# One fused attention and mixer kernel: the first K load ahead of the first Q load, and a new order of work with other engines for some small copies

## The chip, the cores and the metric

The kernel runs on one core of a Trainium2 chip. A core has five engines, each with its own instruction stream, and they meet only through semaphores. PE (TensorE) multiplies, DVE (VectorE), ACT (ScalarE) and POOL (GpSimd) do elementwise work, and SP (SyncE) here only issues transfers (DMAs). POOL also issues transfers. The metric is the device time of one execution in microseconds (us). The times shown are of three runs, and the profile is of one more execution.

## What is computed

Four batches of eight-head attention over 768 tokens with head size 64 are followed by a mixer. Cut to what matters, the reference is:

```python
scores = q @ k.T / 8 - slope[h] * dist          # per batch and head
keep   = (key < 8) | (0 <= query - key < 96)    # 8 global keys, 96 local ones
a      = softmax(where(keep, scores, -1e9))
x      = (a @ v), heads side by side            # 4 x 768 x 512
h      = x.T @ U @ V                            # over tokens, rank 32
u      = x + h.T
out    = u + relu(u @ w_ch1) @ w_ch2            # 512 -> 2048 -> 512
```

All inputs and the output are float32. The kernel computes in float16 with float32 sums.

## The kernel before, in words

**The units of work.** Heads are taken two at a time, so there are 16 pairs, pair p = 4 x batch + head pair. A query block of 128 tokens meets two key blocks: its own, and the one before it with its first 32 keys replaced by the global ones. This second form of K is kept in kO and that of V in vo. A task's name is a short code with the pair's number behind it, and a part behind a dot:

- lk, lq, lv: the loads of K, Q and V (function add_load, L389 to L444). Pair 0's K and Q are loaded as float32 by SP (L416) into stg32, which borrows the memory of the tile sA, and are cast to float16 by Ck0.0, Ck0.1, Cq0.0 and Cq0.1 (L421 to L433). All other loads are issued by POOL and cast on the way (L400, L404, L408).
- TK, TQ: transposes on PE (L518 to L560). EK, EQ: their results copied from PSUM to kT and qT by DVE or ACT. KO: the two copies that make kO (L583 to L609). VC and VG: the two copies that make vo, all keys and then the global ones (L614 to L626).
- SB: the position bias as a matmul, for the first batch alone (L640 to L651). S: the scores. EX: the exponential on ACT (L728). MK: the mask on DVE, for pairs 4 and up. PV: weights times values (L795, L796). RC and NM: the reciprocal and the normalising multiplication on DVE. XC: the cast of x to float16 (L858). UP: transposes and the first step of the mixer (L769 to L779). XE, XU, TE: the middle steps. HM: the last step of the mixer (L890), in a full-array or a half-array form. E0 and E1: the result copied to uT.
- M1a to M1d and RL: the first MLP product and its relu. ZP, ZU, ZW, ZX, ZA, ZB, ZD, ZQ, ZR, ZV, with ZT and ZS: a part of the first MLP in batches 1 to 3 done with seven products for eight. PA and PB: sums on DVE that let the second MLP be done the same way. RS, P1 to P7 and DA to DH: the second MLP and its additions into x_sb. O: the stores by SP.
- w1_0 to w1_3 and w2_0 to w2_3: the weights' loads, 512 KB each, by POOL. mixl: the loads of U and V of the mixer by SP. u16 and vs: copies of these.

**What sets the order.** The list ORDER names every task once, across all engines. A planner (class Planner, method run, L146 to L216) walks the list, gives each task a start time from costs written into the program, and picks the buffer that it uses: three for K and for Q, four for V, eight PSUM banks. The tasks are then emitted by start time. On any one engine this is the order of the list, so what decides on the chip is the list and the buffers; the planner's own times are not run. A task's engine comes from a letter in CFG (A for ACT, D for DVE, P for POOL, S for a transfer by SP): KO, VO (for VC and VG), EK, EQ, XC, TE, XE, E and so on, one letter for each pair.

**What follows for each queue.** An engine takes its tasks strictly in turn. POOL's stream holds the loads and its copies mixed, so a load can't be issued while POOL waits to begin a copy. LANES = 8 (L107) lets at most eight POOL transfers be in flight. V's four buffers are given by PV of an earlier pair, K's and Q's three by TK and TQ.

**Counting.** Each task has a fixed number of instructions on its engine (PV 22, UP 12, a P product 8, KO 2, VC 1). Counting them along the list gives every row of the trace its task.

**Idle matmuls.** Until the first M1a0.0, gaps on PE that the planner foresees are filled with matmuls on zeros (L1201).

Of the kernel before, what the change touches and what calls it, by code (L numbers as in the profile page):

```python
# [10 lines left out]
FP32 = mybir.dt.float32  # L11
# [10 lines left out]
ones2 ones0 wz lq0 iota lk1 ones3 lk0 vz relf rel3 bias1 bias0 bias2 lq1 Ck0.0 Ck0.1 Cq0.0 Cq0.1 SB0.1 lk2 lv0 lq2  # L22
TK0 EK0.1 EK0.0 KO0.0 TQ0 EQ0.0 EQ0.1 SB0.2 lk3 KO0.1 lq3 SB0.0 ones1 S0.0 TK1 EK1 back lv1 S0.2 S0.1 EX0.0 TQ1 EQ1
KO1 lk4 SB1.2 VC0 VG0 lv2 lv3 bias4 EX0.2 EX0.1 lq4 TK2 EK2 KO2 SB1.1 S1.1 EX1.1 S1.2 EX1.2 SB1.0 PV0 RC0 NM0 TQ2
EQ2 TK3 EK3 KO3 S1.0 SB2.1 VC1 VG1 lk5 SB2.2 S2.2 lq5 w1_0 mixl u16 EX1.0 TQ3 EQ3 XC0 EX2.2 SB2.0 S2.0 EX2.0 S2.1
EX2.1 PV1 RC1 VC2 VG2 NM1 VC3 VG3 vs1 vs0 XC1 SB3.1 S3.1 SB3.0 SB3.2 EX3.1 S3.0 S3.2 EX3.0 EX3.2 PV2 RC2 NM2 TK4 EK4
UP0 TQ4 w1_3 KO4 TE0 PV3.0 PV3.1 EQ4 HM0 E00 PV3.2 RC3.0 UP1 NH3.0 TE1 TK5 XC2 TQ5 EK5 KO5 w1_2 HM1 RC3.1 E01 RC3.2
NH3.2 UP3.0 NH3.1 UP3.1 UP3.2 EQ5 lk7 NM3 lv4 TE3 S4.2 UP2 TE2 HM3 E03 M1a0.3 EX4.2 S4.0 HM2 E02 E13 M1c0.3 M1a0.2
M1c0.2 lq6 EX4.0 S5.1 mask1 EX5.1 S4.1 EX4.1 M1d0.3 M1b0.3 RL0.3 lk6 M1d0.2 M1b0.2 RL0.2 w1_1 M1a0.14 VC4 M1a0.0
M1c0.0 M1d0.0 ZS6 mask0 MK4.0 M1b0.14 RL0.14 mask2 M1b0.0 M1a0.15 M1b0.15 TK7 M1a0.9 M1b0.9 EK7 KO7 lq7 M1a0.10  # L30
RL0.15 RL0.0 mask3 RL0.9 MK4.1 TD0 S5.0 EX5.0 w2_2 S5.2 VG4 EX5.2 M1b0.10 MK5.0 lv5 M1a0.11 MK5.1 M1a0.13 M1b0.11
TQ6 RL0.10 MK4.2 EQ6 TK6 RL0.11 M1b0.13 M1a0.7 M1b0.7 RL0.13 EK6 MK5.2 PA0.3 PV4 w2_0 RC4 TQ7 M1a0.6 M1b0.6 RL0.7
EQ7 M1a0.5 w2_1 PB0.3 M1a0.8 vs2 NM4 XC4 UP4 RL0.6 KO6 w2_3 XE4 M1b0.5 RL0.5 M1b0.8 RL0.8 PA0.1 M1a0.1 VC5 PB0.1 VG5
M1c0.1 M1d0.1 XU4 M1a0.4 TE4 HM4 TWa0 TWb0 E04 M1b0.4 RL0.4 M1b0.1 RL0.1 PV5 M1a0.12 M1b0.12 RL0.12 S6.2 RC5 NM5 lk8
RS0.0 S6.1 EX6.1 lq8 PA0.0 P10.0 PB0.0 lq9 PA0.2 mask4 PB0.2 P20.0 S7.0 mask7 TWa1 RS0.1 DA0.0 EX7.0 P10.1 DA0.1
P20.1 TWb1 TK8 mask5 EK8 lv7 mask6 XC5 MK7.0 P30.0 lk9 TQ8 DF0.0 EQ8 P30.1 EX6.2 lk10 P50.0 UP5 DF0.1 XE5 lv6 P60.0
XU5 TE5 P60.1 DB0.1 S6.0 EX6.0 HM5 E05 MK6.0 TK10 EK10 DC0.0 P70.1 lv10 MK6.2 P50.1 KO8 S7.1 EX7.1 S7.2 lq10 RS0.2
DD0.1 lq11 VC6 MK6.1 EX7.2 P10.2 DA0.2 P40.1 VC7 TQ10 EQ10 VG6 PV6 TK9 EK9 MK7.1 VG7 KO9 DB0.0 P70.0 P60.2 MK7.2 PV7
RC6 NM6 TQ9 EQ9 DC0.1 P30.2 lk11 P20.2 O0.1 RC7 lv8 VC8 XC6 UP6 lq14 NM7 XC7 UP7 DD0.0 P40.0 XE6 XU6 XE7 XU7 lk12
TE6 TE7 DB0.2 P70.2 DF0.2 DG0.1 DG0.0 HM6 E06 S8.2 HM7 E07 EX8.2 P50.2 TQ11 E17 KO10 DD0.2 S8.1 EX8.1 S10.2 EX10.2  # L40
S8.0 lk14 EQ11 ZT1 lq13 MK8.2 P40.2 DG0.2 EX8.0 TK11 EK11 KO11 M1a1.12 M1b1.12 RL1.12 M1a1.7 M1b1.7 RL1.7 M1a1.3
M1b1.3 RL1.3 M1a1.8 M1b1.8 DC0.2 MK8.1 RL1.8 M1a1.6 S9.2 EX9.2 S9.1 EX9.1 M1a1.9 MK9.2 M1b1.6 ZP11.6 ZU1.6 ZP21.6
O0.0 MK9.1 RL1.6 M1b1.9 RL1.9 M1a1.13 MK8.0 M1b1.13 ZA1.6 ZS7 lq12 RL1.13 VC10 M1a1.2 M1b1.2 RL1.2 VG8 ZP11.7 PV8
M1a1.4 M1b1.4 RL1.4 M1a1.5 O0.5 lv12 lv9 PA1.2 PB1.2 M1b1.5 RL1.5 PA1.1 PB1.1 VC12 VG12 M1a1.0 M1b1.0 ZU1.7 M1a1.1
M1b1.1 RL1.0 RL1.1 TD1 ZP61.7 ZP61.6 RC8 O0.3 ZP21.7 O0.4 ZW1.7 O0.2 ZW1.6 NM8 XC8 UP8 lv11 MK10.2 ZA1.7 S9.0 EX9.0
# [12 lines left out]
XC12 UP12 XE12 ZP62.4 ZW2.4 ZP32.7 ZD2.7 XU12 TE12 PB2.0 ZP62.5 ZW2.5 ZP52.5 ZP72.4 ZX2.4 ZP52.4 ZB2.4 ZV2.4 HM12
E012 ZP22.5 ZA2.5 ZP72.5 ZR2.7 ZX2.5 ZP42.4 ZR2.4 ZQ2.7 ZQ2.6 ZP32.4 ZD2.4 ZB2.5 ZV2.5 ZQ2.4 M1a2.7 M1b2.7 RL2.7
ZP42.5 ZV2.6 XC14 UP14 M1a2.2 M1b2.2 XE14 XU14 ZP32.5 VC13 VG13 TE14 lv15 ZR2.5 ZV2.7 PA2.3 RL2.2 VC15 M1a2.6 M1b2.6  # L60
RL2.6 ZD2.5 ZQ2.5 PB2.3 PA2.1 HM14 E014 S13.1 RS2.1 P12.1 EX13.1 P22.1 DA2.1 S15.1 EX15.1 RS2.0 S13.0 EX13.0 VG15
PA2.2 P12.0 P22.0 P52.1 P62.1 PB2.2 P52.0 MK13.1 MK13.0 PV13 PB2.1 P32.0 MK15.1 P32.1 DA2.0 P62.0 RC13 DF2.0 DF2.1
DB2.0 DC2.0 S15.0 RS2.2 P32.2 P12.2 EX15.0 P22.2 MK15.2 MK15.0 PV15 P72.0 DA2.2 P62.2 DB2.1 P72.1 NM13 XC13 RC15
NM15 UP13 DD2.0 XC15 UP15 DB2.2 P72.2 XE15 XU15 DF2.2 XE13 XU13 TE13 ZS3.0 P52.2 TE15 ZS3.1 HM13 E013 HM15 E115
DD2.1 P42.0 P42.1 DD2.2 ZP13.6 ZP13.1 ZU3.1 E015 M1a3.8 DG2.0 ZP13.0 ZT3 DC2.2 ZU3.6 M1b3.8 ZP63.6 DG2.1 DC2.1 O2.4
O2.1 ZP63.1 ZU3.0 ZP63.0 ZP23.1 ZA3.1 P42.2 ZW3.6 ZW3.1 ZP73.1 ZW3.0 RL3.8 ZP23.6 ZS3.3 DG2.2 O2.5 ZX3.1 ZP53.1
ZA3.6 ZP13.3 ZU3.3 ZP13.7 ZP73.0 ZU3.7 ZP23.0 O2.3 ZP43.1 ZS3.2 ZR3.1 ZP73.6 ZB3.1 ZX3.0 ZP63.7 ZA3.0 ZW3.7 ZP13.2
ZU3.2 ZV3.1 ZP33.1 ZD3.1 ZP53.0 ZB3.0 ZX3.6 TD3 ZP43.0 ZR3.0 ZP63.3 ZP53.6 ZB3.6 ZV3.6 ZP53.7 ZP33.0 ZD3.0 ZP73.7
ZP43.6 ZP23.7 ZP63.2 ZP23.2 ZW3.3 ZP73.3 ZX3.7 ZP43.7 ZB3.7 ZV3.7 ZP33.7 ZA3.7 ZP33.6 ZR3.6 ZA3.2 ZW3.2 ZD3.7 ZQ3.7
# [34 lines left out]
class Planner:  # L104
# [41 lines left out]
    def run(self, names):  # L146
# [7 lines left out]
        for t in (self.names[n] for n in names):  # L154
# [1096 lines left out]
```

## Time and profile before

| what | value |
|---|---|
| median of 3 runs | 226.46 us (225.27 to 227.72) |
| the profiled execution | 225.36 us |
| its span, first to last instruction | 223.5 us |
| granted TensorE clock, mean | 0.999 |
| PE busy | 216.7 us, 97% |
| DVE busy | 181.8 us, 81% |
| ACT busy | 135.4 us, 61% |
| POOL busy | 92.4 us, 41% |
| chain that ended last, on PE | 84% |

The profiled execution lasts 1.9 us longer than its span. Matmuls overlap and their ends are modelled, so the 97% says that PE has work, and not that matmuls follow each other as closely as they can. For that the starts of neighbouring matmuls have to be compared.

### The profile page before, as it was taken

How to read it: one execution, taken by the hardware profiler on the slowest of the kernel's cores; microseconds unless marked ns; L12 is line 12 of the kernel's file. 1: busy time of each engine (PE TensorE's matmuls, PEld its weight loads, DVE VectorE, ACT ScalarE, POOL GpSimd, SP SyncE). 2: the span in 40 equal slices, each digit the busy share in tenths (PEclk: the TensorE clock that was granted, in tenths of full speed). 3: DMA queues.
4: the chain of work that ended last, by engine and by line, in shares of the span. 5: the costliest groups of instructions: out<-in, count | busy, mean ns of one | idle time of the engine just before them, and what ended most of it. 6: DMA issues, size and time to landing. Idle time of an engine off the chain costs nothing.

```text
span 223.5 us, 5880 instructions
## 1 busy us (share of the span) xinstructions
PE 216.7 (97%) x2414; PEld 159.4 (71%) x2414; DVE 181.8 (81%) x393; ACT 135.4 (61%) x216; POOL 92.4 (41%) x124
## 2 busy tenths in 40 slices
PE   6997999999999999999999999999999999999993
PEld 2665856767888975666788886666698866558883
DVE  6798844798979774799998779799978998988872
ACT  4787898877767376959838446778721157662000
POOL 8888798778974947535105200232000200000000
PEclk9999999999999999999999999999999999999999
DMA  6999999999999994975702943005000006000026
GB/s 174 178 173 159 179 143 176 183 207 173 136 156 79 171 104 146 150 75 35 65 5 32 182 168 112 5 3 35 4 0 3 0 3 235 0 0 3 1 96 236
DMA packets 79067, 22.28 MB, mean 100 GB/s; under 512 B 68384, under 2 KB 76064, under 8 KB 79040
## 3 DMA queue, kind: packets, MB, share of 16 engines
q0 software_dynamic: 68320, 13.24, 70.7%
q1 hardware_dynamic: 10720, 8.66, 12.8%
q8 instruction: 19, 0.31, 0.6%
q14 instruction: 8, 0.07, 0.1%
HBM read 27.46 MB, written 6.29 MB: 151 GB/s over the span
## 4 chain that ended last, share of the span: by engine, by line
PE 84%; DVE 6%; DMA 5%; POOL 1%; issue 1%; ACT 1%; SPq 0%; POOLq 0%; DVEq 0%
PE ps L1136 34%; PE ps L946 21%; PE ps L1015 11%; PE ps L663 4%; PE ps L541 4%; DMA vt<-in_v_dram 4%; PE ps L769 3%; PE ps L796 2%; PE ps L890 2%; PE ps L795 2%; DMA sA<-in_k_dram 2%; PE ps L1128 1%; DVE sA L1097 1%; DVE vo L316 1%; DVE x_sb L834 1%
## 5 line engine op out<-in xcount | busy, mean ns | idle before, releaser
L946 PE MATMUL ps<-uT,w 128*128 128x384 f16 x320 | 56.3, 326 | 0.0
L728 ACT ACTIVATE ep<-ps 128x1024 f16<-128x1024 f32 (+1 forms) x48 | 44.1, 951 | 16.1 <-PE ps L663 15.7
L946 PEld LDWEIGHTS <-w 128*128 128x128 f16 x320 | 30.3, 98 | 19.5 <-issue 0.2
L1136 PEld LDWEIGHTS <-htr 128*128 128x128 f16 x384 | 36.0, 98 | 6.1 <-issue 1.6
L962 ACT ACTIVATE htr<-ps 128x768 f16<-128x768 f32 x40 | 32.0, 813 | 11.7 <-PE ps L946 11.5
L1148 DVE TENSOR_TENSOR x_sb<-x_sb,ps 128x256 f32<-128x256 f32 (+1 forms) x61 | 27.1, 464 | 10.1 <-PE ps L1136 9.4
L1136 PEld LDWEIGHTS <-sA 128*128 128x128 f16 x288 | 27.4, 98 | 3.5 <-issue 0.4
L1136 PE MATMUL ps<-w,sA 128*128 128x256 f16 x192 | 24.1, 273 | 0.0
L1136 PE MATMUL ps<-tB,htr 128*128 128x256 f16 x192 | 23.9, 273 | 0.0
L1136 PE MATMUL ps<-w,htr 128*128 128x256 f16 x192 | 23.3, 273 | 0.0
L408 POOL DMA_DIRECT2D vt<-in_v_dram x16 | 16.7, 1050 | 15.7 <-issue 11.6
L741 DVE TENSOR_TENSOR ep<-ep,mask 128x1024 f16<-128x1024 f16 x24 | 17.5, 734 | 5.0 <-ACT ep L728 5.0
L404 POOL DMA_DIRECT2D stgq<-in_q_dram x24 | 19.9, 852 | 1.0 <-DMA stgk<-in_k_dram 1.0
L404 POOL DMA_DIRECT2D stgk<-in_k_dram x24 | 19.9, 845 | 0.0
L858 POOL CAST x<-x_sb 128x768 f16<-128x768 f32 x8 | 6.9, 866 | 27.0 <-DVE x_sb L834 27.0
L320 POOL COPY vo<-vt 128x660 f16<-128x660 f16 (+1 forms) x14 | 11.2, 808 | 13.7 <-DMA vt<-in_v_dram 13.5
L834 DVE TENSOR_TENSOR x_sb<-ps,rcp 128x768 f32<-128x768 f32 x16 | 15.3, 953 | 0.3
L320 POOL COPY kO<-kT 128x480 f16<-128x480 f16 (+1 forms) x10 | 4.7, 508 | 24.4 <-DVE kT L316 24.4
L663 PE MATMUL ps<-qT,kT 64*128 64x128 f16 x192 | 14.6, 217 | 0.0
L796 PEld LDWEIGHTS <-ep 128*128 128x128 f16 x192 | 12.6, 97 | 2.5 <-issue 1.2
L1033 DVE TENSOR_TENSOR htr<-ps,zu 128x384 f16<-128x384 f32 x24 | 13.0, 551 | 0.8 <-PE ps L1015 0.4
L796 PE MATMUL ps<-vt,ep 128*128 128x65 f16 x192 | 13.6, 193 | 0.0
(125 smaller groups left out, 423.9 us busy)
## 6 DMA issues: line engine op xcount, KB each, us to landing
out_dram<-x_sb SPq DMA_DIRECT2D x23, 256.0 KB, 2.3
w<-in_moe_w_ch_dram POOLq DMA_DIRECT2D x8, 512.0 KB, 7.2
vt<-in_v_dram POOLq DMA_DIRECT2D x16, 192.0 KB, 6.0
stgk<-in_k_dram POOLq DMA_DIRECT2D x24, 96.0 KB, 4.9
stgq<-in_q_dram POOLq DMA_DIRECT2D x24, 96.0 KB, 5.7
vo<-vt SPq DMA_DIRECT2D x5, 165.0 KB, 3.6
stgk<-in_k_dram POOLq DMA_DIRECT2D x3, 192.0 KB, 5.6
stgq<-in_q_dram POOLq DMA_DIRECT2D x3, 192.0 KB, 5.9
```

Of the source, the lines that this page charges most:

```text
L404: nc.gpsimd.dma_start(o[:, i], src[b, h0 + i].rearrange("(n p) d -> p n d", p=P))
L408: nc.gpsimd.dma_start(vt[gv.slot][:, :, :, 0:D], v[b, h0:h0 + 2].rearrange("h (n p) d -> p h n d", p=P),)
L663: nc.tensor.matmul(t[:, hi, j * P:(j + 1) * P], lhs, qt[r, i * P:(i + 1) * P], start=not biased, stop=True, skip_group_check=biased,)
L728: nc.scalar.activation(ep[gep.slot][:, :, lo:512], ps[:, gsc.slot:gsc.slot + 2, lo:512], AF.Exp, scale=qk_scale)
L741: nc.vector.tensor_tensor(ev, ev, mv, ALU.mult)
L796: nc.tensor.matmul(o, e[:, hi, (j + 1) * P:(j + 2) * P], vv[:, hi, i, 0:D1], start=(i == 0), stop=True)
L834: nc.vector.tensor_tensor(xo, pvo()[:, :, :, 0:D], rcp[p % 2].unsqueeze(3).broadcast_to((P, 2, NB, D)), ALU.mult)
L946: nc.tensor.matmul(ps[:, g.slot + half, 0:HS], w1[:, dc, jt * P:(jt + 1) * P], ub[:, dc, half * HS:(half + 1) * HS], start=(dc == flat[0]) ...
L962: nc.scalar.activation(htr[:, jt].rearrange("p (h c) -> p h c", h=2), ps[:, g.slot:g.slot + 2, 0:HS], AF.Relu)
L1015: nc.tensor.matmul(bank(g), a()[:, i], bq[:, i], start=first and i == 0, stop=last and i == 1, skip_group_check=True,)
L1136: nc.tensor.matmul(o, a[:, j, c0 + cols.start:c0 + cols.stop], bq[:, j], start=False, stop=(j == hj - 1), skip_group_check=True,)
L1148: nc.vector.tensor_tensor(o, o, x, ALU.add)
```

## The change

The products are the same, and so are all sizes and types. These things differ:

- SP issues lk0 before lq0. POOL begins with wz and iota, and ones0 to ones3 (the constant column of V's four buffers) come later. lv0 is issued before lk2.
- ORDER is another order of the same tasks throughout.
- Letters in CFG. Copies of K: KO2 and KO7 go from DVE to POOL, KO6 and KO8 from ACT to POOL, KO9 from ACT to SP, KO12 from SP to POOL, KO10 and KO15 from POOL to DVE, KO13 from DVE to ACT. Copies of V: VO4 and VO5 from POOL to DVE, VO8 and VO14 from SP to POOL, VO10 from POOL to SP. EK2 goes from ACT to DVE, EQ1 from DVE to ACT. XC8 goes from DVE to POOL, XC9 from DVE to ACT, XC6 from POOL to ACT, XC10 from ACT to POOL. bias1 and bias2 go from DVE to ACT, vs1 from POOL to ACT. Some of TE, XE, E, EQ, ZQ and ZV change between DVE and ACT.
- HM0, HM1 and HM4 take the half-array form, HM8 the full one.
- The planner has another account of how DVE and POOL wait for each other (function past) and other costs for some tasks. Both act only through the buffers and the gap fillers.
- reli, relb and relc lie in one tile, early. Code for loads of later pairs by SP (DL) and for sums by transfer (AC) is added, but both settings are empty, so nothing of it is emitted.

The start of both lists, the settings that the text speaks of, and the new function:

```diff
 ORDER = """
-ones2 ones0 wz lq0 iota lk1 ones3 lk0 vz relf rel3 bias1 bias0 bias2 lq1 Ck0.0 Ck0.1 Cq0.0 Cq0.1 SB0.1 lk2 lv0 lq2
-TK0 EK0.1 EK0.0 KO0.0 TQ0 EQ0.0 EQ0.1 SB0.2 lk3 KO0.1 lq3 SB0.0 ones1 S0.0 TK1 EK1 back lv1 S0.2 S0.1 EX0.0 TQ1 EQ1
-KO1 lk4 SB1.2 VC0 VG0 lv2 lv3 bias4 EX0.2 EX0.1 lq4 TK2 EK2 KO2 SB1.1 S1.1 EX1.1 S1.2 EX1.2 SB1.0 PV0 RC0 NM0 TQ2
-EQ2 TK3 EK3 KO3 S1.0 SB2.1 VC1 VG1 lk5 SB2.2 S2.2 lq5 w1_0 mixl u16 EX1.0 TQ3 EQ3 XC0 EX2.2 SB2.0 S2.0 EX2.0 S2.1
-EX2.1 PV1 RC1 VC2 VG2 NM1 VC3 VG3 vs1 vs0 XC1 SB3.1 S3.1 SB3.0 SB3.2 EX3.1 S3.0 S3.2 EX3.0 EX3.2 PV2 RC2 NM2 TK4 EK4
+wz iota lk0 lq0 lk1 lq1 ones0 lv0 vz lk2 relf rel3 bias0 bias1 Ck0.1 bias2 SB0.1 lq2 bias4 Ck0.0 mask3 Cq0.1 TK0
+EK0.0 Cq0.0 SB0.2 TQ0 EQ0.1 lk3 EQ0.0 EK0.1 KO0.1 S0.2 EX0.2 lq3 KO0.0 S0.1 EX0.1 ones2 TK1 EK1 KO1 back SB1.0 VC0
+TQ1 EQ1 ones1 lv1 lk4 SB0.0 S0.0 EX0.0 VG0 SB1.1 S1.1 S1.0 lv2 TK2 EK2 PV0 EX1.0 SB1.2 RC0 NM0 EX1.1 TQ2 EQ2 TK3 EK3
+KO3 VC1 VG1 ones3 lv3 XC0 S1.2 EX1.2 KO2 SB2.2 lq4 lk5 lq5 SB2.0 S2.0 EX2.0 S2.2 EX2.2 TQ3 EQ3 SB2.1 PV1 S2.1 EX2.1
+RC1 NM1 VC2 VG2 VC3 VG3 SB3.1 S3.1 EX3.1 SB3.2 SB3.0 w1_0 S3.0 EX3.0 S3.2 EX3.2 TK4 EK4 PV2 RC2 NM2 PV3.0 PV3.1 mixl
...
-M1a1.4 M1b1.4 RL1.4 M1a1.5 O0.5 lv12 lv9 PA1.2 PB1.2 M1b1.5 RL1.5 PA1.1 PB1.1 VC12 VG12 M1a1.0 M1b1.0 ZU1.7 M1a1.1
+ZA1.6 RL1.13 M1a1.9 M1b1.9 RL1.9 PA1.2 PB1.2 lv8 VC8 VG8 M1a1.4 M1b1.4 M1a1.0 M1b1.0 RL1.4 PV8 RL1.0 ZP11.7 O0.3
+ZU1.7 M1a1.1 M1b1.1 RL1.1 ZP61.7 ZW1.7 ZP61.6 ZW1.6 RC8 lv11 NM8 ZP21.7 XC8 UP8 MK9.2 ZA1.7 S9.0 EX9.0 XE8 S11.2
...
-    "EK": "ADADDAADAAADAAAD", "EQ": "DDADADDAAAADDAAD", "KO": "ADDDPPADAAPPSDSP", "HR": "FFRFFRRRRRRRFRRR",
-    "IB": "ADDD", "VS": "PPP", "EKS": "DADADADA", "EQS": "ADDADADA", "VO": "DDDDPPPSSSPPPSSP", "XC": "DPPDDPPDDDAAPPPP"
+    "EK": "ADDDDAADAAADAAAD", "EQ": "DAADADAAAAADDDAD", "KO": "ADPDPPPPPSDPPASD", "HR": "RRRFRRRRFRRRFRRR",
+    "IB": "AAAD", "VS": "PAP", "EKS": "ADDADADA", "EQS": "AADADADA", "VO": "DDDDDDPSPSSPPSPP", "XC": "DPPDDPADPAPAPPPP"
...
+    @staticmethod
+    def past(c, port, kind):
+
+        moved = True
+        while moved:
+            moved = False
+            for a, b, what in port[-24:]:
+                if what == 2:
+                    x = b - (0.14 if kind else 0.1) if a <= c else c
+                else:
+                    x = b - 0.18 if kind == 1 and a + 0.2 < c else c
+                if x > c:
+                    c, moved = x, True
+        return c
```

The settings stand in the program one after another with others between them; here those named in the text are put together.

## The prediction

> **What bounds the kernel now.** I read the page's busy times first, then the matmuls' spacing, then the chain of work that ended last, and then the timelines of POOL and DVE where that chain leaves PE.
>
> ```profile
> PE 216.7 (97%) x2414; PEld 159.4 (71%) x2414; DVE 181.8 (81%) x393; ACT 135.4 (61%) x216; POOL 92.4 (41%) x124
> PE   6997999999999999999999999999999999999993
> DMA  6999999999999994975702943005000006000026
> GB/s 174 178 173 159 179 143 176 183 207 173 136 156 79 171 104 146 150 75 35 65 5 32 182 168 112 5 3 35 4 0 3 0 3 235 0 0 3 1 96 236
> ```
>
> PE is the bound, and the transfers are busy without a break for the first third. Taking the smallest start-to-start distance of each form of matmul (0.162 us at 384 columns, 0.109 at 256, 0.055 at 128), the products need 202.4 us. Idle matmuls at the start take 3.2, the tail behind the last matmul 3.3, the head 1.4. The other 13.2 us are lost between products: 5.9 before 21.66 us, about 6 in changes between full-array and half-array matmuls (75 of them, some 0.1 each, and more at a few), and 0.95 between 101.7 and 104.7. Only the first and the last can be had by a new order. This is the chain at the first place:
>
> ```profile
> 4.84 0.53 ACT stgk L314
> 5.42 0.52 PE ps L541 x6
> ...
> 10.59 8.10 DMA vt<-in_v_dram
> 18.71 0.34 DVE vo L316
> 19.08 1.67 DVE vo L316
> 20.75 0.88 DVE x_sb L834
> 21.66 0.49 PE ps L541 x6
> ```
>
> It ends in V of pair 2: issued at 10.59, landed at 18.69, VC2, VG2, and only then PV2 goes on (the idle row says PE waited 1.12 us for vo). The 8.10 us are a queue: ten POOL loads landed one after another from 6.93 to 17.33. VG2 took 1.67 us where VG1 took 0.50. The other two timelines show why.
>
> ```profile
> 18.97 0.75 POOL L450 DMA_DIRECT2D w<-in_moe_w_ch_dram  x1
> 19.72 0.84 POOL L320 CAST u<-x_sb 128x768 f16<-128x768 f32 x1
> 20.62 1.06 POOL L320 CAST vs<-x_sb 32x384 f16<-32x384 f32 x2
> ```
>
> VG2 begins in w1_0's issue, outlasts u16 and ends 0.19 us behind it. The second place is a DVE chain:
>
> ```profile
> 93.86 0.80 DVE sA L1096
> ...
> 98.97 0.97 DVE x_sb L834
> ...
> 100.03 0.76 DVE x L858
> 100.80 0.71 DVE ep L741
> ...
> 103.10 1.04 DVE sA L1097
> 104.14 0.21 DVE tmp L316
> 104.40 0.34 PE ps L890 x2
> ```
>
> DVE comes to RC8 at 98.71, 3.6 us after PV8 ended (95.1), then runs NM8, XC8, MK10.2, ZA1.7, XE8, PA1.0 and TE8, and PE waits for TE8.
>
> **K first.** SP's two loads of 384 KB landed at 3.75 (Q) and 4.82 (K). Swapped, K lands near 3.75. TK0 can then go at about 4.5 (Ck0.1 behind rel3, which ends at 4.03, plus 0.39) instead of 5.42, and Q's casts at 4.82 instead of 5.2. The exponentials of pair 0 begin near 7.0 instead of 7.82: EK0.0, EQ0.1 and EQ0.0 on ACT (0.49, 0.41, 0.41) and KO0.1 on DVE stand between. So ACT is 0.8 us ahead, and with EK2 moved off it (0.70) and EQ1 and EQ0.1 moved on (0.70, 0.41) it stays some 0.4 to 0.8 ahead. bias1, bias2 and mask3 join ACT in its idle 1.97 us before the first cast; without that cover they would cost 1.1.
>
> What is late next is V2. Ahead of it POOL issues the same eleven transfers, lv0 merely before lk2, and they set its landing. POOL's start gains 0.1 from the two ones. mixl, which shares the transfers until 16.44, waits for `back`, now behind KO1, so some 0.4 later. V2 lands at 18.3 to 18.7. w1_0 can't be issued much before: lq5 is held by the eight in flight (POOL idles 1.01 us before it, until a K load lands). So w1_0 and u16 meet VG2 again. I take VG2's end at 20.6 (20.75 before), bounded by 19.5 (VG2 at VG1's 0.50) and by 21.1 (KO2, 0.94 on POOL, pushes w1_0 and u16 back). Nearest row: VG2 itself.
>
> Behind it the new list has NM1 and TK4 done already, but puts PV3.0 next, which needs VC3 and VG3: 0.32 plus 0.50 to 0.86 from 20.6 on, so 21.4 to 21.8. Before, 23.00 was reached with 0.83 us of PE work more done (UP0 and TQ4, less TK4). Net: 23.00 - 0.83 - 21.8 = 0.4, or up to 1.4 if VG2 is free. XC1 on POOL beside VG3, as before, can take 0.4 back. Then the landings bound the gain from below: w1_0 at 26.19 against M1a0.3 at 27.80 leaves 1.6, lq5 at 23.70 against TQ5 at 25.00 leaves 1.3. **Start: -0.2 (-1.4 to +0.4).**
>
> **The middle.** DVE loses XC8 (0.76) to POOL, XC9 (0.56) and TE9 to ACT; ZS6 and ZS7 (1.0) change places. But PV8 moves 3.57 us of products back and UP8 stays, so that PV8's end to UP8's start, 6.2 us before (95.1 to 101.28), has 2.6. The path needs RC8 0.23, NM8 0.96, XC8 0.85 on POOL and latencies: 2.2. PA1.2 and PB1.2 (1.8 and 1.0) stand ahead of RC8 on DVE and wait for RL1.9. I expect 0.4 us of waiting at UP8 and 0.35 at HM8 (TE8 is again behind PA1.0), where 0.95 was. **Middle: -0.2 (-0.9 to +2.6).** The upper end is the lag of 3.6 us that DVE had, less 0.4 of slack: 3.2 + 0.35 - 0.95.
>
> At this place a rule of the Trainium skill speaks against the change: in "SBUF — State Buffer", Who interferes with whom, VectorE and GpSimd take their shared port pair as a lock for a whole instruction, and "Perfetto Trace Analysis", Optimizing Scalar/DVE Operations, says that moving work between these two might not help. The trace agrees: MK10.2 took 1.21 us beside VG10 on POOL, where its kind has a median of 0.68. By this rule XC8 on POOL holds MK9.2 and ZA1.7 for up to 0.85 us, the middle's term would be +0.1, and the sum below -0.1 in place of -0.4.
>
> **Changes between array forms.** Counted in the lists: 75 before, 78 after, +0.33 at 0.11 each. HM0, HM1 and HM4 become half-array and HM8 full, net two at 0.163: -0.33. Sum 0.
>
> **Copies that move elsewhere.** In 30 to 90 and 110 to 220 us PE waited for nothing but those changes, so a faster copy gains nothing there; it must only not be late. The tightest places, with the tasks ahead in the new list added up by their spacing: V5 is read 6.3 us of products earlier and lv5 moves ahead of lk6, lq7 and w2_2, landing near 40 where PV5 stands at 45; lk6 lands near 41.5 for TK6 at 43.4; KO6, which waits for EK6 until about 44.5, now stands ahead of w2_1 and w2_3, yet these may be issued as late as 48 (P20.0 stands at 54.7, the quickest weight load took 5.55 us, and one issue takes 0.78); VC11 behind lv15's landing ends near 114 for PV11 at 118. On SP, KO9's two transfers stand ahead of the first stores and VC8, VG8 and KO12 are gone; nothing on PE reads a store. All hidden; uncovered, each costs PE what it is late. The last product, its addition (0.42) and the last store (1.99) are the same: 0.
>
> **Sum.** -0.2 - 0.2 + 0 = -0.4 on the profiled execution's 225.36: 225.0. The median lies 1.1 above that execution, and two of four executions lie at 225.3. I put the forecast between: 225.4.
>
> **Rivals.**
>
> - VG2 escapes u16, and DVE is on time at RC8: -1.4 - 0.8 = -2.2, so 223.2. For it: DVE is idle before V2 (0.93) and the new list leaves less ahead of it. Against: w1_0 and VC2 are let go by the same landing. 0.22.
> - K's lead is wasted: VG3 also meets XC1 and PV3.0 waits longer, +0.4, and the middle stays: 225.8. For it: VG3 took 0.86 beside XC1. 0.13.
> - Slower, by one wait: DVE is as late at RC8 as before. PE stalls there for 3.2, the middle's upper end: 225.36 - 0.2 + 2.6 = 227.8 (228.9 from the median). It decides once RC8 comes over 0.4 us after PV8. For it: the measured lag of 3.6. Against: PA1.1, PB1.1 and MK10.2 stand earlier and XC8 is gone. 0.15.
>
> **How the numbers follow.** Forecast 0.50, rivals 0.22, 0.13, 0.15. The likeliest gives 225.4, its own range 224.2 to 227.0 (the two scales of 1.1 us and the terms' middles). The whole range runs from 223.1, the first rival, to 227.6, which leaves out the slower one and little else. One per cent, 2.3 us, is about what a measurement here can tell from no change. The first rival is beyond it in most of its cases, with a little of the forecast: faster 0.21. The third, with a little: slower 0.16. The rest 0.63.
>
> **What would show it.** K's cast near 3.8, the first exponential near 7.0, V2's landing at 18.3 to 18.7, VG2 over 1.2 us with u16 beside it, M1a0.3 at 27.3 to 27.8, UP8 within 0.6 us of its place, the last matmul 3.3 us before the end. I am wrong if V2 lands before 17.5, if VG2 takes 0.5, if PE waits over 0.3 us anywhere from 30 to 90 or behind 110, or if POOL holds a w2 load until PE waits for it.

## The result, and the profile after

The changed kernel takes 228.99 us (median of 12 runs, 227.40 to 229.65), the kernel before 226.67 us beside it (12 runs, 225.27 to 227.72). The ratio is 1.0104, 95% interval 1.0072 to 1.0135: slower by 2.3 us, where 225.4 was forecast and 227.6 was the end of the range. The profiled execution of after took 227.91 us, with a span of 226.1 and a granted clock of 1.00.

The page of after, its busy times and one of its groups (busy, mean ns of one, then PE's idle time just before them and what ended it):

```profile
PE 218.2 (96%) x2432; PEld 160.1 (71%) x2432; DVE 182.9 (81%) x389; ACT 137.5 (61%) x218; POOL 94.4 (42%) x128
L1167 PE MATMUL ps<-w,sA 128*128 128x256 f16 x192 | 23.9, 273 | 0.9 <-DVE sA L1133 0.9
```

PE is the bound as before, and it waits in a new place: 0.9 us for a sum on DVE (PB1.0).

To see where the time went, take each task's start less an allowance for all the products ahead of it in its list: their smallest spacing, as in the prediction, and here also some 0.11 us for each of before's changes of array form. A task's allowance is the same in every kernel. What is left is how late PE is at that task, in us, and only the differences between kernels are read from it. Two kernels of the experiments and a second profile of after (there called after again) stand beside it.

| how late PE is at | before | after | after, second profile | best4 | u16_and_w1 |
|---|---|---|---|---|---|
| M1a0.3 (27.80 us before) | 7.89 | 8.79 | 9.35 | 8.96 | 7.17 |
| PV8 | 8.17 | 9.07 | 10.61 | 9.23 | 7.44 |
| PV9 | 8.96 | 9.46 | 11.01 | 9.68 | 8.22 |
| P31.1 | 8.98 | 10.97 | 12.22 | 9.89 | 8.24 |
| P43.2, the last product | 9.46 | 11.47 | 12.72 | 10.37 | 8.73 |
| from P43.2's start to the span's end | 4.42 | 5.05 | 5.04 | 4.60 | 4.44 |
| span | 223.5 | 226.1 | 227.4 | 224.6 | 222.8 |

From before to after: the start +0.90, from there to PV8 0.0 (in the second profile +1.0), the middle from PV8 to PV9 -0.40, from PV9 to P31.1 +1.49, then 0.02, and the closing +0.63. The sum is 2.64; the spans differ by 2.65.

**The start.** The chain of work that ended last in after, from V2's copies on:

```profile
18.14 0.96 DVE x_sb L865
19.10 0.25 DVE vo L339
19.38 0.57 DVE vo L339
19.94 1.36 issue
21.30 0.95 DVE vo L339
22.27 0.33 DVE vo L339
22.65 0.19 PE ps L826
```

and POOL's timeline beside it (start, duration):

```profile
19.13 0.78 POOL L481 DMA_DIRECT2D w<-in_moe_w_ch_dram  x1
19.87 0.86 POOL L343 CAST u<-x_sb 128x768 f16<-128x768 f32 x1
20.64 0.54 POOL L343 CAST vs<-x_sb 32x384 f16<-32x384 f32 x1
21.09 0.96 POOL L889 CAST x<-x_sb 128x768 f16<-128x768 f32 x1
```

The chain cuts VG2 and VC3 short. As single rows of DVE's timeline they are:

```profile
19.38 2.00 DVE L339 COPY vo<-vt 32x660 f16<-32x660 f16 x1
21.30 0.94 DVE L339 COPY vo<-vt 128x660 f16<-128x660 f16 x1
```

VG2 runs from 19.38 to 21.37, 2.0 us where it took 1.67 before, beside u16 and vs0; VC3 takes 0.94 beside XC1, where it took 0.32. VG3 ends at 22.60, and PV3.0, now right behind PV2, waits for it. The copies were slow in before too: VC2, VG2, VC3 and VG3 took 3.17 us together there, against 3.58 here and 3.33 in the second profile of after. But in before UP0 and TQ4 stood between PV2 and PV3.0, and VG3, which ended at 22.75, was hidden behind them. K's load lands at 3.94 and the first exponential begins at 7.33 (7.82 before): K first works, and nothing is left of it at V2.

**From 112 to 117 us.** DVE's timeline in before, where POOL was idle, and in after:

```profile
111.03 0.55 DVE L1101 TENSOR_TENSOR htr<-htr 128x768 f16<-128x768 f16 x1
111.50 0.55 DVE L1102 TENSOR_TENSOR sA<-htr,sA 128x768 f16<-128x768 f16 x1
111.97 0.41 DVE L1148 TENSOR_TENSOR x_sb<-x_sb,ps 128x256 f32<-128x256 f32 x1
```

```profile
112.50 0.42 DVE L1179 TENSOR_TENSOR x_sb<-x_sb,ps 128x256 f32<-128x256 f32 x1 [0.41 <-PE ps L1167]
112.84 1.15 DVE L1132 TENSOR_TENSOR htr<-htr 128x768 f16<-128x768 f16 x1
113.91 1.08 DVE L1133 TENSOR_TENSOR sA<-htr,sA 128x768 f16<-128x768 f16 x1
114.92 1.61 DVE L1132 TENSOR_TENSOR htr<-htr 128x768 f16<-128x768 f16 x1
116.45 0.66 DVE L1133 TENSOR_TENSOR sA<-htr,sA 128x768 f16<-128x768 f16 x1
```

```profile
112.13 3.46 POOL L343 COPY vo<-vt 128x660 f16<-128x660 f16 x4 [3.17 <-DMA vt<-in_v_dram]
115.54 1.16 POOL L343 COPY kO<-kT 128x480 f16<-128x480 f16 x2
```

PB1.3 and PB1.0 are two sums each. They take 0.55 us a sum in before and 0.66 to 1.61 in after, exactly while POOL makes the copies VC15, VG12, VC11, VG11 and KO12 back to back; POOL had stood 3.17 us waiting for V15. P31.1, which needs PB1.0, begins at 117.17, 1.09 us behind its place. The addition into x_sb, which reads PSUM, keeps its 0.42.

**The last w2 loads.** POOL's waits in after from 36 to 62 us, and PE's waits behind 30 us in the second profile of after (us in all, times, longest):

```profile
POOL kO L343 <- ACT kT L337: 4.5, 1, 4.5
```

```profile
PE ps L1167 <- DMA w<-in_moe_w_ch_dram: 1.0, 1, 1.0
PE ps L1167 <- DVE sA L1133: 0.8, 1, 0.8
```

KO6 on POOL waits 4.5 us for EK6, and w2_1 and w2_3 stand behind it: issued at 47.43 and 48.16 (40.53 and 42.24 before), the last landing at 56.70 (53.40). P20.0 begins at 56.15, and its second half needs that load. P20.0 takes 1.04 us in before, 1.19 in the first profile of after and 2.18 in the second (landing at 58.25), so the load costs 0.15 us and 1.14.

### The profile page after: what moved, and what is told of

It reads as the page before. It is cut to its first block, busy times and chain, and to the rows that moved or that the text cites. A ratio compares the mean times of both kernels' runs of the same rounds, so it can differ in the third digit from the quotient of the medians.

```text
span 226.1 us, 5927 instructions
## 1 busy us (share of the span) xinstructions
PE 218.2 (96%) x2432; PEld 160.1 (71%) x2432; DVE 182.9 (81%) x389; ACT 137.5 (61%) x218; POOL 94.4 (42%) x128
## 4 chain that ended last, share of the span: by engine, by line
PE 87%; DVE 6%; issue 2%; DMA 2%; ACT 1%; SPq 0%; DVEq 0%
PE ps L1167 32%; PE ps L977 23%; PE ps L1046 12%; PE ps L694 5%; PE ps L572 3%; PE ps L800 2%; PE ps L827 2%; DMA sA<-in_q_dram 2%; PE ps L826 2%; PE ps L1159 1%; PE ps L921 1%; DVE vo L339 1%; DVE x_sb L865 1%; PE ps L1246 1%; DVE kT L339 1%
## 5 line engine op out<-in xcount | busy, mean ns | idle before, releaser
L993 ACT ACTIVATE htr<-ps 128x768 f16<-128x768 f32 x40 | 31.2, 812 | 11.9 <-PE ps L977 11.6
L889 POOL CAST x<-x_sb 128x768 f16<-128x768 f32 x9 | 8.0, 888 | 45.5 <-DVE x_sb L865 43.3
L772 DVE TENSOR_TENSOR ep<-ep,mask 128x1024 f16<-128x1024 f16 x24 | 16.8, 711 | 4.5 <-ACT ep L759 4.5
L343 POOL COPY vo<-vt 128x660 f16<-128x660 f16 (+1 forms) x12 | 9.6, 809 | 13.5 <-DMA vt<-in_v_dram 13.3
L343 POOL COPY kO<-kT 128x480 f16<-128x480 f16 (+1 forms) x16 | 7.9, 531 | 12.6 <-DVE kT L339 8.1
```

What stands on the lines that cost most here:

```text
L343: nc.gpsimd.tensor_copy(dst, src)
L772: nc.vector.tensor_tensor(ev, ev, mv, ALU.mult)
L993: nc.scalar.activation(htr[:, jt].rearrange("p (h c) -> p h c", h=2), ps[:, g.slot:g.slot + 2, 0:HS], AF.Relu)
```

## The experiments

The theory: a copy on POOL holds up DVE's copies and sums between SBUF tiles, and that makes the stalls at 20 and at 116 us. Its rivals: DVE is late there by the new order alone; the swap of the loads delays the start; the new array forms do. Each kernel was timed against before on its own chip; the ratios below are to that. The expectations use "idle matmuls" for the fillers on zeros.

### 1. Before with K first

```diff
-ones2 ones0 wz lq0 iota lk1 ones3 lk0 vz relf
+ones2 ones0 wz lk0 iota lk1 ones3 lq0 vz relf
```

> The kernel before with K's first load issued ahead of Q's, and everything else in its old order. Theory (copies and load issues on GpSimd hold up VectorE's copies and sums; the swap of the loads itself is harmless): K lands about 1 us earlier, the first exponential comes at or a little ahead of 7.82 us, M1a0.3 starts within 0.4 us of 27.80 us, time within 0.5 us of before. Rival (the swap delays the start): M1a0.3 near 28.7 us and about 0.9 us more in all.

Measured: 225.77 us against 225.59, ratio 1.0005 (0.9989 to 1.0021). M1a0.3 at 27.67. The swap is harmless, and by itself worth nothing: VG2 ends at 20.62 as ever (20.75 before). In this profile Q landed at 5.46 and the first exponential came at 8.47, later than expected.

### 2. After with Q first

```diff
-wz iota lk0 lq0 lk1
+wz iota lq0 lk0 lk1
```

> The kernel after with Q's first load issued ahead of K's again, and nothing else undone. Theory: the start's loss of 0.9 us is made by the copies around 19 to 22 us, so it stays; as the new plan now meets a K that is late, the time is 0 to 1 us above after. Rival (the swap delays the start): M1a0.3 comes back from 28.70 to about 27.8 us and the time falls by 0.9 us.

The planner's rule that the second of these loads waits for the first goes with it. Measured: 228.51 us, ratio 1.0134 (1.0098 to 1.0169); M1a0.3 at 29.54, 0.84 later. The swap isn't what costs the start.

### 3. After with five copies off POOL, four of them at 107 to 117 us

```diff
-"KO": "ADPDPPPPPSDPPASD"   "VO": "DDDDDDPSPSSPPSPP"
+"KO": "ADPDPPPPPSDPSASD"   "VO": "DDDDDDPSPSSPSSPS"
```

> The kernel after with the copies VC12, VG12, VC15, VG15 and KO12 on no GpSimd: V12, V15 and K12's bf16 copies go to SyncE's choice (issued as transfers) in place of GpSimd. Theory (GpSimd's copies stretch PB1.3 and PB1.0 from 1.02 to 2.2 us each, and that is the wait at P31.1): PB1.3 and PB1.0 fall towards 1.1 to 1.5 us, the wait of 1.09 us at 116.05 us goes, the time falls by 0.7 to 1.1 us. Rival (VectorE is late there by the new order): both sums may be short, but P31.1 starts no earlier, 0 us.

The copies are VC12, VG12, VC15, the pair KO12, and VG15, which ran at 133 us. Measured: 226.98 us, ratio 1.0053 (1.0027 to 1.0078), about half of after's loss. POOL's last copies (VC11, VG11) end at 112.30, and DVE's timeline is whole again:

```profile
114.26 0.55 DVE L1132 TENSOR_TENSOR htr<-htr 128x768 f16<-128x768 f16 x1
114.72 0.55 DVE L1133 TENSOR_TENSOR sA<-htr,sA 128x768 f16<-128x768 f16 x1
115.19 0.55 DVE L1132 TENSOR_TENSOR htr<-htr 128x768 f16<-128x768 f16 x1
115.66 0.55 DVE L1133 TENSOR_TENSOR sA<-htr,sA 128x768 f16<-128x768 f16 x1
```

P31.1 doesn't wait. The order of DVE's work is that of after, so the rival of the order falls for this stall. In this profile P20.0 still took 1.99 us (1.04 in before), so the w2 loads' wait is a part of what is left.

### 4. Copies put into before, at two places

```diff
+XX  = nc.vector.memset(relc, 0.0)                            # second kernel only
+XX0 to XX7 = nc.gpsimd.tensor_copy(relc, w1[:, 0, 0:384])    # eight, behind PA1.3 in the list
```

> The kernel before with eight copies on GpSimd that nothing needs (128x384, one of the weights' parts into the table that is done with), let go by PA1.3, so that they run from about 111 to 115 us beside PB1.3 and PB1.0, where GpSimd was idle. They add no work for TensorE, VectorE or ScalarE. Theory (copies on GpSimd stretch these sums): PB1.3 and PB1.0 go from 1.02 us to 1.6 to 2.2 us, their rows from 0.55 to 0.8 to 1.6 us; P31.1 had 1.3 us of room behind PB1.0, so it waits 0.2 to 0.9 us and the time rises by 0.2 to 0.9 us. Rival (the sums are long in after for another reason): both stay within 0.1 us of 1.02 us and the time does not change.

The first kernel missed its aim. Nothing made the copies wait, and they ran up to 108.7 us, ahead of the sums. PB1.3 and PB1.0 stayed at 1.02 and the time at 225.76 us, ratio 1.0002 (0.9984 to 1.0020). So eight copies on POOL cost nothing where no such sum lies beside them. The second kernel lets them go by a write on DVE:

> The kernel before with the eight idle copies on GpSimd again (128x384 each), now let go by a memset on VectorE right behind PA1.3 of the table they write, so that they do run from about 111.2 us beside PB1.3 and PB1.0. The memset adds 0.1 to 0.2 us to VectorE. Theory: PB1.3 and PB1.0 go from 1.02 us to 1.6 to 2.2 us each, P31.1 (1.3 us of room) waits 0 to 0.9 us; time up by 0 to 0.9 us. Rival: both sums stay within 0.1 us of 1.02 us.

DVE's and POOL's timelines of the second:

```profile
111.61 0.49 DVE L1100 TENSOR_TENSOR htr<-htr 128x768 f16<-128x768 f16 x1
112.03 0.85 DVE L1101 TENSOR_TENSOR sA<-htr,sA 128x768 f16<-128x768 f16 x1
112.80 0.41 DVE L1151 TENSOR_TENSOR x_sb<-x_sb,ps 128x256 f32<-128x256 f32 x1
...
113.73 0.85 DVE L1100 TENSOR_TENSOR htr<-htr 128x768 f16<-128x768 f16 x1
114.51 0.85 DVE L1101 TENSOR_TENSOR sA<-htr,sA 128x768 f16<-128x768 f16 x1
```

```profile
111.76 6.22 POOL L1109 COPY relc<-w 128x384 f16<-128x384 f16 x8 [8.24 <-DVE relc L1107]
```

Each sum beside a copy takes 0.85 in place of 0.55, with no other change but the small write; the first, begun ahead of them, is not longer. PB1.3 rose to 1.26 and PB1.0 to 1.63, the lower side of what was expected, and within P31.1's room: 225.93 us, ratio 1.0004 (0.9983 to 1.0024). The mechanism is shown in both directions: the copies taken away in experiment 3, and put in here. Nothing in the program makes these sums wait for these copies, so the engines don't meet through semaphores alone, as the section on the cores has it. That the delay must be longer than the room before PE loses anything is shown too.

### 5. The start of after, five tries

u16, vs0 and XC1 to ScalarE; then u16 on POOL ahead of lq5; then these with experiment 3, with the old array forms, and with PV3.0 and PV3.1 behind TK5.

```diff
-"U16": "P"  "VS": "PAP"  "XC": "DPP..."   SB3.2 SB3.0 ... PV3.1 mixl u16 UP0 ... TE0 XC1 XC2
+"U16": "A"  "VS": "AAP"  "XC": "DAP..."   mixl u16 SB3.2 SB3.0 ... EX3.2 XC1 ... TE0 XC2      # pool_20
+"U16": "P"  "VS": "AAP"  "XC": "DAP..."   lk5 mixl u16 lq5 ... vs1 XC1 TE0 XC2                # start
+start, and the letters of experiment 3                                                     # both
+both, and "HR": "FFRFFRRRRRRRFRRR"                                                         # both_hr
+U16, VS and XC as in after; letters of 3; HR as above; lk5 mixl u16 lq5; TK5 PV3.0 PV3.1   # best2
```

> The kernel after with u16, vs0, vs1 and XC1 on ScalarE in place of GpSimd, and mixl's and u16's issue put after EX3.1. Theory (VG2's 2.0 and VG3's wait come from GpSimd's work beside them): VG2 falls from 2.0 to 0.8 to 1.2 us, VG3 ends 0.8 to 1.2 us earlier than 22.60, the wait of 0.56 us at PV3.0 goes, M1a0.3 starts 0.5 to 1.0 us ahead of 28.70 us, the time falls by 0.5 to 1 us. Rival (the start is late by the array forms of HM0 and HM1 and by the order): M1a0.3 within 0.2 us of 28.70, 0 us.

> The kernel after with GpSimd free beside VG2 and VG3: u16 stays on GpSimd but goes between K5's and Q5's load, vs0 and XC1 go to ScalarE with vs1 (XC1 behind vs1), so that HM0 is not behind a full ScalarE as it was with u16 there too. Theory (GpSimd's copies beside VG2 and VG3 cost the start 0.9 us): VG2 0.7 us and VC3 0.3 us, no wait at PV3.0, HM0 waits 0.3 us at most, M1a0.3 starts 0.7 to 1.1 us ahead of 28.70 us, the time is 0.7 to 1.1 us under after. Rival (the start is late by the half forms of HM0 and HM1 and the new order): M1a0.3 within 0.3 us of 28.7 us, 0 us.

> Both edits together: GpSimd free beside VG2 and VG3, and V12's, V15's and K12's copies issued as transfers by SyncE. Theory: the two stalls are apart in place and both go, so the time is 1.7 to 2.2 us under after, some 0.2 to 0.4 % above before to level with it. Rival (a stall taken away is met again by the next late engine): less than 1.3 us under after.

> As both edits together, and HM0, HM1, HM4 in the whole array and HM8 in the half one again, as before. Theory (changes of array form cost some 0.1 us each and these nearly cancel): within 0.4 us of both edits. Rival (the half form of HM0 and HM1, with a switch of 0.17 to 0.18 us behind each, is what delays the start): 0.5 to 0.8 us under both edits.

> The kernel after, unchanged, beside the next three on one chip, so that they can be compared with it there. All theories: 0.7 to 1.4 % above before, P31.1 waits 0.9 to 1.1 us, PV3.0 0.4 to 0.8 us.

> The kernel after with four edits: V12's, V15's and K12's copies issued by SyncE; PV3.0 and PV3.1 (with RC3.0 and NH3.0) behind UP0, TQ4 and TK5, as before; u16 on GpSimd ahead of Q5's load, clear of VG2; the array forms of before for HM0, HM1, HM4 and HM8. Theory (two stalls beside GpSimd's copies and the forms make the loss): no wait over 0.3 us at PV3.0 and P31.1, the time 1.8 to 2.6 us under after, within 0.3 % of before or under it. Rival (what is taken away comes back elsewhere): less than 1.2 us under after.

| kernel | us | ratio (95%) | VG2 | M1a0.3 | idle matmuls at 19 to 30 us |
|---|---|---|---|---|---|
| pool_20 | 227.90 | 1.0114 (1.0075 to 1.0152) | 0.68 | 28.55 | 21 |
| start | 228.65 | 1.0108 (1.0072 to 1.0145) | 0.71 | 29.18 | 18 |
| both | 226.63 | 1.0032 (1.0010 to 1.0053) | 0.71 | 29.70 | 18 |
| both_hr | 226.59 | 1.0027 (1.0010 to 1.0045) | 0.70 | 28.86 | 16 |
| after again | 228.39 | 1.0120 (1.0091 to 1.0149) | 0.83 | 29.25 | 0 |
| best2 | 226.90 | 1.0058 (1.0041 to 1.0075) | 0.83 | 29.91 | 28 |

VG2 shrank as the theory says, and the start gained at most 0.15 us. Three things hid the answer, and none was reckoned with. The planner foresaw gaps there and filled them with 16 to 28 matmuls on zeros, some 0.06 us each, so that PE was busy with nothing when its data came. And the start differs from execution to execution: V1 landed at 15.54 in after and at 17.09 in "start", where PV1 waited 1.2 us. And P20.0 went on waiting for the w2 loads: it took 1.98 us in "start" and 1.54 in "both", 1.04 in before. "both" and "both_hr" agree within their intervals, so the array forms don't decide. best2 has PV3.0 behind UP0 and TQ4 again, as before, but V1 was late and 28 matmuls on zeros stood there too, so the order's own share of the start's loss is not separated.

### 6. The start again, without such fillers

```diff
-            if t.eng == PE and t.start <= until and CFG.get("warm", True):
+            if t.eng == PE and t.start <= min(until, 15.0) and CFG.get("warm", True):
```

For after ("start3") with u16, vs0 and XC1 on ScalarE, XC1 behind TE0. For before, one move at a time: u16 on POOL ahead of lq5 (still with fillers), u16 on ScalarE behind EX3.1, and that with w1_3 issued ahead of vs1, vs0 and XC1.

> The kernel after with u16, vs0 and XC1 on ScalarE (XC1 behind TE0), so that GpSimd does nothing beside VG2 and VG3 but issue w1_0, and with no idle matmuls behind 15 us of the plan. Theory: VG2 0.7 us in place of 2.0 us, VC3 0.3, M1a0.3 starts 0.6 to 1.0 us ahead of 28.70 us if the loads land as in after, the time falls by 0.5 to 1 us. Rival: M1a0.3 within 0.3 us of 28.7 us, 0 us.

> The kernel before with one move on GpSimd: u16 goes ahead of Q5's load, so that it runs before VG2 starts and not beside it (u16 19.72 to 20.55 us, VG2 19.08 to 20.75 us). Theory (VG2's 1.67 us is stretched by the copy beside it): VG2 falls to 0.7 to 1.0 us, the wait of 1.29 us inside PV2 falls to 0.3 to 0.6 us, M1a0.3 starts 0.6 to 0.9 us ahead of 27.80 us, the time falls by 0.5 to 0.9 us. Rival (VG2 is long because V2's rows have just landed, or by its own work): VG2 stays over 1.4 us, 0 us.

> The kernel before with u16 on ScalarE, behind EX3.1, in place of GpSimd, and with no idle matmuls behind 15 us of the plan (before has none there). Theory (the copy beside VG2 stretches it to 1.67 us and PV2 waits for it): VG2 0.7 us, the wait of 1.29 us inside PV2 falls to 0.3 to 0.6 us, M1a0.3 0.6 to 0.9 us ahead of 27.80 us, the time 0.4 to 0.9 us under before. Rival (VG2 is long by itself): VG2 over 1.4 us, 0 us.

> The kernel before with u16 on ScalarE behind EX3.1, and GpSimd's issue of w1_3 ahead of vs1, vs0 and XC1, so that these copies run some 0.75 us later, behind VC3 and most of VG3. Theory (VG2 and VG3 are long only beside a copy on GpSimd): VG2 0.5 us, VC3 and VG3 0.3 to 0.6 us each, PV3.0 waits 0.4 us at most, M1a0.3 starts 0.7 to 1.2 us ahead of 27.80 us, and the time falls 0.4 to 1.1 us under before. Rival (the wait moves on to the next late copy): M1a0.3 within 0.4 us of 27.8 us, 0 us.

start3: VG2 0.68 and VC3 0.31, M1a0.3 at 28.24, 0.46 ahead of after (1.0 ahead of its second profile) though the first scores came 0.16 later; XC1, late on ScalarE, now makes UP1 wait 0.65. 228.57 us, ratio 1.0089 (1.0060 to 1.0119): the rows moved as expected, the time less; P20.0 took 1.62 here.

u16 ahead of lq5 in before: VG2 0.32, but VG1 went from 0.50 to 1.42 beside u16, PV1 waited 0.84, and 30 matmuls on zeros stood in front of HM0. 227.22 us, ratio 1.0073 (1.0055 to 1.0090), a miss.

u16 on ScalarE: here are DVE and then POOL. A row of two copies is VC2 and VG2, then VC3 and VG3.

```profile
18.34 0.86 DVE L315 COPY vo<-vt 128x660 f16<-128x660 f16 x2 [0.46 <-DMA vt<-in_v_dram]
19.99 1.89 DVE L315 COPY vo<-vt 128x660 f16<-128x660 f16 x2
```

```profile
19.87 1.05 POOL L319 CAST vs<-x_sb 32x384 f16<-32x384 f32 x2
20.88 0.82 POOL L857 CAST x<-x_sb 128x768 f16<-128x768 f32 x1
```

VG2 fell from 1.67 to 0.50, VG3 rose from 0.85 to 1.29 beside XC1, the wait went from PV2 to PV3.0 (1.27), M1a0.3 came at 27.82: 226.02 us, ratio 1.0008 (0.9973 to 1.0043). The stall moved to the next pair of neighbours. With w1_3 ahead the copies clear VG3 as well:

```profile
18.81 0.69 DVE L315 COPY vo<-vt 128x660 f16<-128x660 f16 x2 [0.77 <-DMA vt<-in_v_dram]
20.30 0.84 DVE L315 COPY vo<-vt 128x660 f16<-128x660 f16 x2
```

```profile
20.27 0.74 POOL L449 DMA_DIRECT2D w<-in_moe_w_ch_dram  x1 [0.44 <-DMA vt<-in_v_dram]
21.05 1.05 POOL L319 CAST vs<-x_sb 32x384 f16<-32x384 f32 x2
22.06 0.82 POOL L857 CAST x<-x_sb 128x768 f16<-128x768 f32 x1
```

VG2 0.32, VG3 0.49, no wait over 0.3 us there, M1a0.3 at 27.07, 0.73 ahead of before, although the first scores came 0.56 later. 225.12 us against 225.63, ratio 0.9972 (0.9943 to 1.0001). This is the fastest kernel seen, and its interval just touches no change.

### 7. The w2 loads, and all places together

"w2_early" moves w2_0, w2_1 and w2_3 right behind w2_2. "best3" is start3, experiment 3, w2_early and the old array forms. "best4" has u16 and vs0 on ScalarE without the late fillers, experiment 3 and the old array forms, leaves XC1, vs2 and KO7 on POOL, and moves KO6 behind the last two loads:

```diff
-w2_2 RC4 mask7 PV5 vs2 TQ7 EQ7 NM4 KO7 w2_0 XC4 KO6 w2_1 M1a0.5 M1b0.5 RC5 RL0.5 w2_3 lk8
+w2_2 w2_0 w2_1 w2_3 RC4 mask7 PV5 vs2 TQ7 EQ7 NM4 KO7 XC4 KO6 M1a0.5 M1b0.5 RC5 RL0.5 lk8        # w2_early
+w2_2 RC4 mask7 PV5 vs2 TQ7 EQ7 NM4 KO7 w2_0 XC4 w2_1 M1a0.5 M1b0.5 RC5 RL0.5 w2_3 KO6 lk8        # best4
```

> The kernel after with w2_0, w2_1 and w2_3 right behind w2_2 on GpSimd, ahead of vs2, KO7, XC4 and KO6, and nothing else. Theory (K6's copy on GpSimd holds the last two w2 loads 6 us, and P20.0 waits for them): the last w2 load lands by 54 us, P20.0 does not wait, the time falls by 0.3 to 1.1 us. Rival (these loads are hidden anyway, or lie behind the DMA engines and not behind GpSimd's queue): landing within 1 us of 56.7 us, 0 us.

> The kernel after with all four undone: u16, vs0 and XC1 off GpSimd at 20 us and no idle matmuls there; V12's, V15's and K12's copies issued by SyncE; the w2 loads in one go; the array forms of before for HM0, HM1, HM4 and HM8. Theory (these are the whole loss): 2.3 to 3.2 us under after, from 0.2 % above before to 0.4 % under it. Rival (a part of the loss is elsewhere): over 0.5 % above before.

> The kernel after with u16 and vs0 on ScalarE and no idle matmuls behind 15 us of the plan; V12's, V15's and K12's copies issued by SyncE; KO6 behind the last two w2 loads on GpSimd, vs2 and KO7 left where they are; the array forms of before for HM0, HM1, HM4 and HM8. Theory: P31.1 and P20.0 do not wait, VG2 0.7 us, PB0.3 1.1 us; 2.0 to 3.0 us under after, within 0.3 % of before. Rival (each stall taken away comes back beside the next copy): over 0.5 % above before.

w2_early: the last load landed at 55.53 (by 54 was expected), and P20.0 didn't wait. But vs2 and KO7 now ran at 44 to 47 us, beside PB0.3 and V5's copies:

```profile
43.82 0.94 DVE L1131 TENSOR_TENSOR htr<-htr 128x768 f16<-128x768 f16 x1
44.68 1.35 DVE L1132 TENSOR_TENSOR sA<-htr,sA 128x768 f16<-128x768 f16 x1
45.95 1.59 DVE L338 COPY vo<-vt 128x660 f16<-128x660 f16 x2
```

```profile
44.27 1.33 POOL L498 TENSOR_TENSOR vs<-x_sb 32x384 f16<-32x384 f32 x1
45.57 2.15 POOL L342 COPY kO<-kT 128x480 f16<-128x480 f16 x4
```

PV5 waited 0.97: 229.61 us, ratio 1.0153 (1.0106 to 1.0200). best3 has the same fault in part (PB0.3 1.52): 227.67, ratio 1.0062 (1.0035 to 1.0090). best4: 226.32 us, ratio 1.0013 (0.9985 to 1.0041), where after stood at 1.0120 (1.0091 to 1.0149): some 1.1%, 2.4 us, came back. Neither P31.1 nor P20.0 waits. VC3 is still at 0.94 beside XC1, and PV3.0 waits 0.96.

## Why the prediction was wrong

- **K first** landed as worked out (3.94, TK0 at 4.60). The first exponential came at 7.33, not at 7.0, and in other executions up to 8.4. That nothing is left of the lead at V2 was right.
- **Start, -0.2, at most +0.4: wrong.** It came to +0.9. V2's landing (18.80, foreseen at 18.3 to 18.7) and the meeting of VG2 and u16 were foreseen; the size wasn't. VG2's end was bounded by 21.1 and came at 21.37; vs0 lay beside it as well as u16. VC3 was taken at 0.32 and took 0.94 beside XC1. So VG3 ended at 22.60 and not at 21.4 to 21.8. The nearest row, VG2's own, was no bound: VG2 took 0.32 to 0.83 us in the runs that kept u16 away from it, and up to 2.00 beside u16.
- **Middle, -0.2:** -0.40 from PV8 to PV9, inside its bounds. The slower rival, DVE as late at RC8 as ever, didn't come: RC8 began 0.04 us behind PV8's end. Nor did XC8 on POOL hold MK9.2 or ZA1.7, as the prediction's own rule had it: they took 0.68 and 0.56, and it was XC8 that got longer, 1.22 us where 0.85 was taken.
- **Array forms, 0:** both_hr against both shows no more than the intervals. PE's lateness still grew by some 0.4 from PV9 to P31.1 beside the wait there, and that is no change of form. Ahead of ZP31.6 PE lost 0.23: ZP31.6 needs ZB1.6 on DVE, and ZB1.6 stood behind ZV1.7, which took 0.83 us (0.26 in before) beside two issues of Q13's load on POOL and the start of VC12; in experiment 3, where VC12 isn't on POOL, it took 0.68. The rest, 0.15, lies in the small products ahead of P21.0, and its cause is open. DVE's row and the issues on POOL beside it:

```profile
106.37 0.83 DVE L1105 TENSOR_SCALAR htr<-htr 128x384 f16<-128x384 f16 x1
```

```profile
105.32 1.65 POOL L432 DMA_DIRECT2D stgq<-in_q_dram  x2 [0.40 <-PE ps L572]
```

- **"All hidden": this step failed, and with it the forecast.** For the copies that move, the prediction asked only whether each is done in time for its own reader. VC11 ended at 114.58, as foreseen, in good time for PV11, which began at 121.94. What it held up on the way was DVE: PB1.3 and PB1.0 at 2.2 us each, and PE for 1.1. Experiment 3 took that away, and experiment 4 made such sums longer in before. Two of the prediction's own signs of being wrong came with it: a wait over 0.3 us behind 110, and a w2 load that POOL held until PE waited. The rule was in the prediction, weighed at XC8 alone. The Trainium skill's page "SBUF — State Buffer", Who interferes with whom, says that a VectorE instruction with two SBUF inputs contends with a GpSimd instruction that reads SBUF. The trace agrees: a sum with both inputs in SBUF goes from 0.55 to between 0.66 and 1.61 us, and one with an input in PSUM keeps its 0.42. Read so, the rule called for every SBUF sum on DVE to be held against every copy on POOL.
- **KO6 ahead of the w2 loads** was seen, and passed as hidden with 5.55 us from issue to landing, the quickest row. That row was w1_2's. w2_3's own row in before was 11.2, and the five weight loads issued from 32 to 49 us in after had a median of 8.5. The margin was taken from the wrong row.
- **Tail, 0:** +0.63, all of it behind the last store's landing; see below.

What stays open: the start. start3 and u16_and_w1 show that the wait there follows the copies beside V's; that this is the whole +0.9 isn't shown, since before's copies were slow as well, the new list has less work between PV2 and PV3.0, best4 is still 1.07 late there and every start differs by up to 1 us.

## What to carry over

When a small copy is moved to GpSimd, ask not only whether it is done in time: lay it beside what VectorE does in the same microseconds, and count a sum of two SBUF tiles there as 1.2 to 2.9 times as long, as here (0.66 to 1.61 us for 0.55). A load issued by GpSimd is as late as the copy queued ahead of it. A stall that is taken from one pair of neighbours often turns up at the next, so only the last wait before PE, and not the row, says what a move is worth.

## What the runs showed of the hardware beyond that

- The copies on GpSimd get longer too: in after VC15 and VG12 took 0.73 each, VG11 0.94 and VC11 1.10; KO12's pair took 1.16, where a pair of its form (KO4) took 0.85.
- The first six transposes took 0.49 us in one execution and 0.80 in another of the same order (after, and the kernel of experiment 3). Matmuls of 128 columns started 0.055 us apart in the first and 0.107 in the second, where the closer spacing began at 7.33 us. The trace's record of the granted clock, which reads 1.00, begins at 4.51 us in after and at 7.32 in experiment 3; the mean of 1.00 counts the time ahead of the record as full, and so doesn't show the difference. With the landings this moves the first scores of the new order between 6.71 and 7.92 us.
- The closing differs. From the last store's landing to the span's end it takes 0.9 us in before and 1.5 in both profiles of after. SyncE then waits for its stores one after another, about 0.07 us each, as the trace's semaphore events show: in before the wait for the last store is the last of them, in after three follow it, and the first of these comes 0.48 us behind it. In experiment 3 three follow too, all 0.07 us apart, and it takes 1.1. What makes the 0.48 is not shown.
- Not the copies alone: an issue of a load on POOL beside it goes with a longer row on DVE too. ZV1.7 and its like (128x384, one SBUF input) took 0.24 to 0.26 us in 138 rows of the twenty profiles with nothing of POOL beside them, and 0.62 to 0.69 in nine with such issues alone. The two sums of PB kept their 0.55 beside issues (111 rows).
